# Seven of eight experts: tokens turned to columns, and results turned back, by VectorE's 32x32 block transposes instead of TensorE's, with the rows taken by way of DRAM

## The chip, the cores and the metric

The kernel runs on one core of one Trainium2 chip. The metric is the device time of one execution in microseconds (us); the figure for the kernel before is the median of 3 runs.

## What is computed

An attention readout gives 4352 tokens of 512 features. They go through a gated feed-forward layer, and its result, `x` below, through a layer of 8 experts, each of which takes 544 tokens (`cap`):

```python
logits = x @ w_gate                      # 4352 x 8
order = np.argsort(-logits.flatten())
for idx in order:                        # best scores first
    tok, e = int(idx) // E, int(idx) % E
    if assigned[tok] >= 0 or counts[e] >= cap: continue
    assigned[tok] = e; counts[e] += 1
for e in range(E):
    mask = assigned == e
    h = np.maximum(x[mask] @ w1[e], 0.0)   # 512 -> 1024
    out[mask] = h @ w2[e]                  # 1024 -> 512
```

## The kernel before

Phases 1 and 2 (attention, gated layer, its output projection, and the routing) leave two things: the rows of `x` in DRAM (`yd`, 4352 x 512) and a table `idx` with, for each expert, the numbers of its 544 tokens in five blocks (four of 128 and one of 32). The change touches phase 3, the experts, one after the other.

Products are taken with split operands: each operand is a high and a low part, and three matmuls (high x high, high x low, low x high) stand for one. So every operand of a matmul is cast once by ScalarE (ACT, the high part) and subtracted once by VectorE (DVE, the low part); `split` does both.

For one expert:
- **gather** (L959 on): GpSimd (POOL) reads each block of rows by an indirect DMA into `row` (5 buffers). TensorE (PE) turns each block into columns with 4 transposes into PSUM, `pt` (L976; 20 for an expert). ACT and DVE split `pt` into `thi` and `tlo`.
- **up** (L981 on): for each of 8 feature blocks and two token ranges (256 and 288 columns) PE does 12 matmuls into `pu` (L994, 3 PSUM banks); ACT writes `uhi` (L996) and DVE `ulo` (L997). Here the next expert's gather is run in steps (`beside`).
- **down** (L1015 on): the tokens from 256 on are computed features by tokens, 4 feature blocks of 24 matmuls of 288 columns each, into `pd` (L1026), and copied by ACT to `sw`. The first 256 tokens are computed tokens by features, 2 blocks of 24 matmuls of 512 columns (L1038).
- **swapped** (L1045 on): PE turns `sw` back to rows with 12 transposes (L1052). **scatter** copies a block of rows to `o` (L1007, ACT or DVE by turns) and POOL stores the rows at their places in the output by an indirect DMA (L1008).
- **weights**: `load` (L853) issues 512 KB of weights on SyncE's (SP) queue into `raw` (3 buffers), and `weight` splits it into a ring of 12 `w` tiles (L66 on ACT, L67 on DVE). An expert takes four such tiles for `w1` and four for `w2`.

A scheduler orders the instructions of each engine in this phase by simulated times. Each engine and each queue then works through its own list in order, and waits on semaphores.

Of the kernel before, what the change touches and what calls it, by code (L numbers as in the profile page):

```python
# [9 lines left out]
F32 = mybir.dt.float32  # L10
F32R = mybir.dt.float32r
BF16 = mybir.dt.bfloat16
I32 = mybir.dt.int32
# [4 lines left out]
OP = mybir.AluOpType  # L18
# [6 lines left out]
DM, FF = 512, 1536  # L25
E, F2 = 8, 1024
CAP = N // E
# [18 lines left out]
def some(steps, n):  # L46
    for _ in range(n):
        next(steps, None)


def whole(steps):
    for _ in steps:
        pass


class Program:
# [923 lines left out]

    def up(self, x, w, beside):  # L981
# [4 lines left out]
        for f in range(8):  # L986
# [12 lines left out]
            if 0 < f < 7:  # L999
                some(beside, 1)  # L1000
        whole(beside)
        return hi, lo

    def scatter(self, e, i, n, pd):
        nc = self.nc
        o = self.op.tile([128, DM], F32, name="o", bufs=4)
        (nc.vector.tensor_copy if i % 2 else nc.scalar.copy)(o[:n], pd[:n])  # L1007
        st = nc.gpsimd.indirect_dma_start(  # L1008
            out=self.out, in_=o[:n], in_offset=None,
            out_offset=bass.IndirectOffsetOnAxis(ap=self.idx[:n, 5 * e + i:5 * e + i + 1], axis=0))  # L1010
        for other in self.stores:
            self.tc.declare_no_dep(st.ins, other.ins, reason="rows of other tokens")
        self.stores.append(st)

    def down(self, e, x, w):  # L1015
# [3 lines left out]
        sw = self.op.tile([128, 4, CAP - T], F32, name="sw", bufs=1)  # L1019
        for fb in range(4):  # L1020
# [8 lines left out]
            nc.scalar.copy(sw[:, fb], pd)  # L1029
# [12 lines left out]
        if e < E - 1:  # L1042
            self.swapped(e, sw)
# [12 lines left out]
    def phase3(self):  # L1056
        tc, nc, a = self.tc, self.nc, self.a
        with ExitStack() as ctx:
# [10 lines left out]
            self.turned = self.turn  # L1069
            for e in range(E):  # L1070
                x2 = self.up(x, w1, self.gather(e + 1, more) if e + 1 < E else iter(()))
# [5 lines left out]
                self.down(e, x2, w2)  # L1077
# [3 lines left out]
    def run(self, out):  # L1081
        tc, nc = self.tc, self.nc
        self.out = out
        with ExitStack() as ctx:
# [6 lines left out]
            self.yd = dp.tile([N, DM], F32, name="yd")  # L1091
            with ExitStack() as pools, ExitStack() as first:
                self.phase1(pools, first)
                self.phase2(pools, first, ctx)
# [3 lines left out]
def layout(i):  # L1098
# [20 lines left out]
    w1 = i["moe2_w1"].reshape(E, 4, 128, 4, 256)  # L1119
    o["w1"] = c(w1.transpose(0, 3, 2, 1, 4).reshape(E, 4, 128, 1024))  # L1120
    w2 = i["moe2_w2"].reshape(E, 4, 2, 128, DM)
# [16 lines left out]
    o["ident"] = np.eye(128, dtype=f)  # L1138
    o["cst"] = np.concatenate([np.asarray(parts[n], f) for n, _, _ in CONSTS], 1)
# [16 lines left out]
```

## Time and profile before

| | |
|---|---|
| median of 3 runs | 1313.41 us (1312.94 to 1313.56) |
| the profiled execution | 1317.34 us |
| its span, first to last instruction | 1315.5 us |
| mean granted clock of TensorE | 0.978 |
| busy in the span | PE 1253.0 us, weight loads (PEld) 1006.5, DVE 803.9, ACT 557.6, POOL 230.1 |

The profiled execution is 3.93 us above the median. Shares are averages over phases with different limits; the experts take about the last 430 us. Where a row gives a time, it counts from the start of the span.

### The profile page before, as it was taken

The page shows a single profiled execution, that of the slowest core. Times are in us where ns is not written, and L with a number is a line of the kernel's source. Part 1 is how long each engine was busy: PE and PEld are TensorE (multiplying, and loading weights), DVE is VectorE, ACT ScalarE, POOL GpSimd, SP SyncE. Part 2 cuts the span into 40 slices and gives each one's busy share as a digit, 9 for nine tenths or more (in the row PEclk, how much of TensorE's full clock was granted, in tenths as well). Part 3 has the DMA queues.
Part 4 walks back from the last instruction along what each step waited for, and adds up shares of the span by engine and source line. Part 5 has one row for each costly group of instructions (what it writes and reads, how often), then busy time and mean ns, then how long its engine had stood idle before and what let it go on. Part 6 is the DMA issues. An engine that isn't in the chain of part 4 may idle for free.

```text
span 1315.5 us, 21466 instructions
## 1 busy us (share of the span) xinstructions
PE 1253.0 (95%) x8351; PEld 1006.5 (77%) x8351; DVE 803.9 (61%) x1673; ACT 557.6 (42%) x975; POOL 230.1 (17%) x205
## 2 busy tenths in 40 slices
PE   5888999999999999999999999979999999999997
PEld 2556768777775555877777777759999999999996
DVE  7999998778553332469889989745335344253220
ACT  4878876787642232431212121224334334343221
POOL 5754451222100000000000000033112112021011
PEclk9788999999999999999999999989999999999999
DMA  7554566345454574643333333347335244253000
GB/s 265 176 166 148 169 190 175 105 157 161 135 145 132 163 198 131 227 137 113 120 106 119 107 115 110 105 133 226 119 102 164 90 139 139 69 170 131 1 35 34
DMA packets 132885, 178.50 MB, mean 136 GB/s; under 512 B 9648, under 2 KB 99888, under 8 KB 132784
## 3 DMA queue, kind: packets, MB, share of 16 engines
q1 hardware_dynamic: 127152, 159.30, 38.6%
q0 software_dynamic: 5632, 17.83, 4.1%
q8 instruction: 66, 1.08, 0.4%
q14 instruction: 35, 0.29, 0.1%
HBM read 129.38 MB, written 47.71 MB: 135 GB/s over the span
## 4 chain that ended last, share of the span: by engine, by line
PE 56%; issue 22%; DVE 11%; DMA 4%; POOL 4%; ACT 2%; SPq 0%; POOLq 0%; ACTq 0%; DVEq 0%
PE pp L274 20%; PE pp L893 17%; PE ps_x L251 4%; PE pu L994 3%; PE ps_s L313 2%; POOL out L1008 2%; DMA raw<-w 2%; PE pd L1026 2%; PE ps_l L313 2%; POOL row L968 2%; PE pd L1038 1%; DVE slo L262 1%; PE ps_s L658 1%; DVE hlo L871 1%; DVE cvc L93 1%
## 5 line engine op out<-in xcount | busy, mean ns | idle before, releaser
L893 PE MATMUL pp<-w,hhi 128*128 128x512 f32 x816 | 261.7, 398 | 0.0
L994 PE MATMUL pu<-thi,w 128*128 128x256 f32 (+1 forms) x1024 | 209.0, 291 | 0.9 <-DVE ulo L997 0.6
L893 PEld LDWEIGHTS pp<-w,hhi 128*128 128x128 f32 x816 | 151.5, 188 | 33.8 <-issue 2.5
L274 PE MATMUL pp<-ahi,shi 128*128 128x512 f32 x384 | 159.2, 415 | 9.1 <-ACT shi L258 4.5
L994 PEld LDWEIGHTS pu<-thi,w 128*128 128x128 f32 x1024 | 166.3, 189 | 1.6 <-DVE ulo L997 0.8
L893 PE MATMUL pp<-w,hlo 128*128 128x512 f32 x408 | 162.4, 398 | 1.3 <-DVE hlo L871 1.3
L262 DVE TENSOR_TENSOR slo<-ps_x,shi 64x512 fp32r<-64x512 f32 x192 | 132.0, 687 | 40.3 <-ACT shi L258 37.2
L274 PE MATMUL pp<-ahi,slo 128*128 128x512 f32 x384 | 151.3, 403 | 3.4 <-DVE slo L262 3.4
L274 PE MATMUL pp<-alo,shi 128*128 128x512 f32 x384 | 153.8, 401 | 0.7 <-POOL alo L67 0.7
L994 PE MATMUL pu<-tlo,w 128*128 128x288 f32 (+1 forms) x512 | 148.8, 291 | 0.0
L881 ACT CAST hhi<-hlo 128x768 fp32r<-128x768 f32 x68 | 53.4, 833 | 221.1 <-PE pp L893 212.2
L67 DVE TENSOR_TENSOR w<-raw,w 128x1024 fp32r<-128x1024 f32 x56 | 68.8, 1228 | 117.8 <-ACT w L66 111.1
L280 DVE TENSOR_TENSOR ht<-pp,sg 128x512 f32<-128x512 f32 (+1 forms) x108 | 71.3, 660 | 113.1 <-PE pp L274 80.3
L258 ACT CAST shi<-ps_x 64x512 fp32r<-64x512 f32 x192 | 111.5, 581 | 57.9 <-PE ps_x L251 52.3
L997 DVE SCALAR_TENSOR_TENSOR ulo<-pu,uhi 128x256 fp32r<-128x256 f32 (+1 forms) x128 | 56.0, 439 | 100.4 <-ACT uhi L996 93.7
L274 PEld LDWEIGHTS pp<-ahi,shi 128*128 128x128 f32 x384 | 73.5, 192 | 46.4 <-ACT sg L278 9.7
L1026 PE MATMUL pd<-uhi,w 128*128 128x288 f32 x512 | 107.5, 298 | 0.0
L278 ACT ACTIVATE sg<-pp 128x512 f32<-128x512 f32 (+1 forms) x108 | 62.0, 575 | 94.0 <-PE pp L274 92.9
L996 ACT ACTIVATE uhi<-pu 128x256 fp32r<-128x256 f32 (+1 forms) x128 | 50.8, 398 | 117.6 <-PE pu L994 104.0
L994 PEld LDWEIGHTS pu<-tlo,w 128*128 128x128 f32 x512 | 96.9, 189 | 0.1
L274 PEld LDWEIGHTS pp<-ahi,slo 128*128 128x128 f32 x384 | 73.8, 192 | 27.0 <-DVE slo L262 9.4
L893 PEld LDWEIGHTS pp<-w,hlo 128*128 128x128 f32 x408 | 76.8, 188 | 18.0 <-DVE hlo L871 1.7
(235 smaller groups left out, 2231.2 us busy)
## 6 DMA issues: line engine op xcount, KB each, us to landing
raw<-w SPq DMA_DIRECT2D x64, 512.0 KB, 3.3
hlo<-hd SPq DMA_DIRECT2D x34, 768.0 KB, 4.3
hd<-ht SPq DMA_DIRECT2D x96, 256.0 KB, 2.6
hraw<-hd SPq DMA_DIRECT2D x144, 128.0 KB, 3.2
raw<-wgv SPq DMA_DIRECT2D x24, 512.0 KB, 5.0
yd<-ys SPq DMA_DIRECT2D x32, 256.0 KB, 3.3
xt<-xt SPq DMA_DIRECT2D x12, 512.0 KB, 5.4
xn<-xn SPq DMA_DIRECT2D x12, 512.0 KB, 4.5
```

What stands on the lines that cost most here:

```text
L67: lo_engine.tensor_tensor(lo, src, hi.bitcast(F32), OP.subtract)
L251: nc.tensor.matmul(ps[:, 256 * g:256 * g + 256], ss[:, 2 * g + z, :], wf[:, ws, :, 2 * g + z, :], start=i == 0, stop=i == 2)
L258: nc.scalar.copy(hi[r[z], b], banks[z][q])
L262: nc.vector.tensor_tensor(lo[r[z], b], banks[z][q], hi[r[z], b].bitcast(F32), OP.subtract)
L274: nc.tensor.matmul(pp, w(ws, k, m), xx[:, k, :], start=i == 0, stop=i == 3 * kt - 1)
L278: nc.scalar.activation(sg, pg, AF.Silu)
L280: nc.vector.tensor_tensor(ht, pv, sg, OP.mult)
L881: nc.scalar.copy(hi[:, q], raw[:, q])
L893: nc.tensor.matmul(py, x[:, f, :], wo[f // 2][:, f % 2, ws, :], start=i == 0, stop=i == 3 * NF - 1)
L994: nc.tensor.matmul(pu, wf[:, ws, k, cs], x[xs][:, k, q], start=i == 0, stop=i == 11)
L997: nc.vector.scalar_tensor_tensor(lo[:, f, q], pu, 0.0, hi[:, f, q].bitcast(F32), op0=OP.max, op1=OP.subtract)
L1026: nc.tensor.matmul(pd, wf[:, ws, f % 2, 128 * fb:128 * fb + 128], xs[:, f, T:], start=i == 0, stop=i == 23)
```

## The change

For experts 1 to 7, `fetch` takes the place of `gather`. The rows are gathered as before, but then SP stores them to a DRAM buffer `xg` and reads them back by 20 smaller DMAs into another arrangement: partition t of quarter z holds, for the tokens t, t+32, ..., the 128 features of quarter z. On this DVE's block transpose, which turns each 32x32 block in its place, gives columns. They have their features in another order within a 128-row tile; the host permutes the rows of `w1` for experts 1 to 7 to match.

For experts 0 to 6, DVE's block transpose also takes `pd` of the 288-column part straight from PSUM to `sw`, where 32 tokens then stand with a quarter row (128 features) on each partition. POOL stores them as 9 indirect DMAs of quarter rows, by a table `idx4` (4 times the row number, plus the quarter) that is made once. The host permutes the columns of `w2`, and the copy to `o` undoes this for the tokens below 256. Expert 0's gather and expert 7's way back stay as they were.

```diff
+    def fetch(self, e, x):
+        nc = self.nc
+        hi, lo = [self.tp.tile([128, 4, CAP], F32R, name=n) for n in ("thi", "tlo")]
+        x[:] = hi, lo
+        xg = self.xg[e - 1]
+        blocks = [(slice(128 * i, min(128 * i + 128, CAP)), min(128, CAP - 128 * i)) for i in range(5)]
+        for i, (q, n) in enumerate(blocks):
+            row = self.tp.tile([128, DM], F32, name="row", bufs=5)
+            nc.gpsimd.indirect_dma_start(
+                out=row[:n], out_offset=None, in_=self.yd,
+                in_offset=bass.IndirectOffsetOnAxis(ap=self.idx[:n, 5 * e + i:5 * e + i + 1], axis=0))
+            nc.sync.dma_start(xg[q], row[:n])
+        yield
+        four = []
+        for q, n in blocks:
+            four.append(self.tp.tile([128, DM], F32, name="row", bufs=5).rearrange("p (b c) -> p b c", c=128))
+            for z in range(4):
+                nc.sync.dma_start(four[-1][32 * z:32 * z + 32, :n // 32],
+                                  xg[q, 128 * z:128 * z + 128].rearrange("(b t) c -> t b c", t=32))
+        yield
+        for (q, n), t in zip(blocks, four):
+            turned = self.tp.tile([128, 4, 128], F32, name="turned")
+            nc.vector.transpose(turned[:, :, :n].rearrange("p f (b c) -> p f b c", c=32),
+                                t[:, :n // 32].rearrange("p b (f c) -> p f b c", c=32))
+            self.split(hi[:, :, q], lo[:, :, q], turned[:, :, :n], nc.vector)
+            yield
@@ up
-            if 0 < f < 7:
+            if f in (1, 4):
                 some(beside, 1)
-        whole(beside)
@@ scatter
-        (nc.vector.tensor_copy if i % 2 else nc.scalar.copy)(o[:n], pd[:n])
+        (nc.vector.tensor_copy if i % 2 else nc.scalar.copy)(
+            o[:n].rearrange("p (q f c) -> p f q c", q=4, c=32), pd[:n].rearrange("p (f q c) -> p f q c", q=4, c=32))
@@ down
+        turned = sw.rearrange("p f c -> p (f c)").rearrange("p (b c) -> p b c", c=128)
...
-            nc.scalar.copy(sw[:, fb], pd)
+            if e == E - 1:
+                nc.scalar.copy(sw[:, fb], pd)
+            else:
+                nc.vector.transpose(turned[:, :, 32 * fb:32 * fb + 32], pd.rearrange("p (b c) -> p b c", c=32))
+            some(beside, 1)
+        if e < E - 1:
+            quarters = self.out.rearrange("n (q c) -> (n q) c", q=4)
+            for b in range((CAP - T) // 32):
+                i = 5 * e + 2 + b // 4
+                self.store(quarters, turned[:, b], self.idx4[:, b % 4, i:i + 1])
         for t in range(2):
...
             self.scatter(e, t, 128, pd)
-        if e < E - 1:
-            self.swapped(e, sw)
+            some(beside, 1)
+        whole(beside)
@@ phase3
+            four, self.idx4 = [self.op.tile([128, 4, 5 * E], I32, name=n, bufs=1) for n in ("four", "idx4")]
+            quarter = self.op.tile([128, 1], F32, name="quarter", bufs=1)
+            nc.sync.dma_start(quarter, a["quarter"])
+            for z in range(4):
+                for b in range(4):
+                    nc.sync.dma_start(four[32 * z:32 * z + 32, b], self.idx[32 * b:32 * b + 32])
+            nc.vector.tensor_scalar(self.idx4, four, 4.0, quarter, op0=OP.mult, op1=OP.add)
```

`store` is the second half of the old `scatter` under its own name.

The lists of the engines move with it. On PE, at the end of an expert in steady state (`pd` of the 512-column part, then `pu` of the next expert), the list before reads:

```order
L1038 MATMUL pd<-w,uhi 128x512 x2
L1038 MATMUL pd<-w,ulo 128x512
L1052 MATMUL pt<-ident,sw 128x128 x8
L994 MATMUL pu<-thi,w 128x256
L994 MATMUL pu<-tlo,w 128x256
L994 MATMUL pu<-thi,w 128x256 x2
```

and the list of the changed kernel, at the same place:

```order
L1079 MATMUL pd<-w,uhi 128x512 x2
L1079 MATMUL pd<-w,ulo 128x512
L1023 MATMUL pu<-thi,w 128x288
L1023 MATMUL pu<-tlo,w 128x288
L1023 MATMUL pu<-thi,w 128x288
L1023 MATMUL pu<-thi,w 128x256
L1023 MATMUL pu<-tlo,w 128x256
```

The 8 transposes of `sw` are gone. The first two `pu` groups of the next expert (all 12 matmuls of one, 9 of the other) have moved ahead, into this expert's `down`, so only the 3 last matmuls of the second stand behind `pd` before the third `pu` begins.

On DVE, in expert 0, the list before, from the second `ulo`'s neighbours on (`w` is the low part of a weight tile):

```order
L997 SCALAR_TENSOR_TENSOR ulo<-pu,uhi 128x256
L67 TENSOR_TENSOR tlo<-pt,thi 128x4x32
L67 TENSOR_TENSOR tlo<-pt,thi 128x4x128
L997 SCALAR_TENSOR_TENSOR ulo<-pu,uhi 128x256
L67 TENSOR_TENSOR w<-raw,w 128x1024
L997 SCALAR_TENSOR_TENSOR ulo<-pu,uhi 128x288
L67 TENSOR_TENSOR w<-raw,w 128x1024
```

and of the changed kernel:

```order
L1026 SCALAR_TENSOR_TENSOR ulo<-pu,uhi 128x256
L67 TENSOR_TENSOR tlo<-pt,thi 128x4x32
L1117 TENSOR_SCALAR idx_9633<-four,quarter 128x160
L1026 SCALAR_TENSOR_TENSOR ulo<-pu,uhi 128x256
L1026 SCALAR_TENSOR_TENSOR ulo<-pu,uhi 128x288 x2
L1005 STREAM_TRANSPOSE turned<-row 128x512
L1026 SCALAR_TENSOR_TENSOR ulo<-pu,uhi 128x256
L67 TENSOR_TENSOR tlo<-turned,thi 128x4x128
L1005 STREAM_TRANSPOSE turned<-row 128x512
```

The block transposes of expert 1 (`turned`) now stand between the `ulo` of expert 0, and the weights' low parts have moved behind them.

On SP the list before is, through all experts, only loads of weights. In the changed kernel, in steady state (`xg_89` is one expert's DRAM buffer):

```order
L994 DMA xg_89<-row 128x512 x2
L853 DMA raw<-w 128x1024 x3
L994 DMA xg_89<-row 128x512
L853 DMA raw<-w 128x1024
L994 DMA xg_89<-row 128x512
L853 DMA raw<-w 128x1024
L1000 DMA row<-xg_89 32x4x128 x4
L994 DMA xg_89<-row 32x512
```

The loads of weights now stand in one queue with stores that wait for a gather, and with the reads back.

## Rows read from the trace of the kernel before

**Rows 1.** Windows: busy us (instructions) of each engine, PE clock, DMA share, GB/s
```profile
894.00:915.00 21.00, 20.21 (x158) 19.77 (x159) 13.87 (x23) 11.58 (x22) 6.96 (x6) 1.00 0.82 271
1102.00:1154.00 52.00, 52.00 (x370) 49.37 (x370) 20.58 (x31) 19.73 (x37) 9.54 (x10) 1.00 0.39 125
```

**Rows 2.** Timeline of POOL: start, duration, instruction [idle before <- releaser]
```profile
1043.05 1.01 POOL L1008 DMA_INDIRECT out<-o,idx  x1 [25.69 <-ACT o L1007]
...
1102.21 0.98 POOL L1008 DMA_INDIRECT out<-o,idx  x1 [0.31 <-issue]
1103.49 0.98 POOL L1008 DMA_INDIRECT out<-o,idx  x1 [0.30 <-issue]
...
1146.88 1.01 POOL L1008 DMA_INDIRECT out<-o,idx  x1 [25.70 <-ACT o L1007]
```

**Rows 3.** Timeline of PE in one steady expert, same columns; xN is N in a run
```profile
1091.77 0.62 PE L1038 MATMUL pd<-w,uhi 128*128 128x512 f32 x2
...
1098.72 0.62 PE L1038 MATMUL pd<-w,uhi 128*128 128x512 f32 x2
...
1100.53 0.40 PE L994 MATMUL pu<-thi,w 128*128 128x256 f32 x2
...
1101.23 0.40 PE L994 MATMUL pu<-thi,w 128*128 128x256 f32 x2
...
1105.04 0.28 PE L994 MATMUL pu<-thi,w 128*128 128x256 f32 x1
1105.16 0.60 PE L976 MATMUL pt<-ident,row 128*128 128x128 f32 x4
...
1105.72 0.30 PE L994 MATMUL pu<-tlo,w 128*128 128x288 f32 x1
...
1131.28 0.43 PE L1026 MATMUL pd<-uhi,w 128*128 128x288 f32 x2
...
1132.48 0.56 PE L1026 MATMUL pd<-uhi,w 128*128 128x288 f32 x3
```

**Rows 4.** Tile pt: xcount, ns min/median/max, first and last start us, forms
```profile
L976 PE MATMUL pt<-ident,row x160: 220/272/477, 884.7 to 1223.6; 128*128 128x128 f32 x128, 32*128 32x32 f32 x32
...
L1052 PE MATMUL pt<-ident,sw x96: 270/272/273, 944.7 to 1304.8; 128*128 128x128 f32 x64, 128*32 128x128 f32 x32
```

**Rows 5.** DVE's groups by shape: count | busy us, mean ns | idle before, releasers
```profile
L67 DVE TENSOR_TENSOR w<-raw,w 128x1024 fp32r<-128x1024 f32 x56 | 68.8, 1228 | 117.8 <-ACT w L66 111.1 <-PE pu L994 5.7
...
L997 DVE SCALAR_TENSOR_TENSOR ulo<-pu,uhi 128x288 fp32r<-128x288 f32 x64 | 29.2, 456 | 56.5 <-ACT uhi L996 51.3 <-issue 3.3 <-ACT o L1007 1.9
...
L204 DVE STREAM_TRANSPOSE aT<-sT 128x512 f32<-128x512 f32 x12 | 8.5, 705 | 3.9 <-POOL sT L193 3.3 <-POOL alo L67 0.6
...
L1007 DVE COPY o<-pd 128x512 f32<-128x512 f32 x8 | 5.5, 686 | 24.8 <-PE pd L1038 24.8
```

**Rows 6.** DMA issues: count, size, median us from issue to landing
```profile
raw<-w SPq DMA_DIRECT2D x64, 512.0 KB, 3.3
...
hraw<-hd SPq DMA_DIRECT2D x144, 128.0 KB, 3.2
...
yd<-ys SPq DMA_DIRECT2D x8, 64.0 KB, 2.9
```

**Rows 7.** Timelines of POOL and of PE where expert 0 begins
```profile
881.12 1.15 POOL L968 DMA_INDIRECT row<-yd,idx  x1 [1.41 <-issue]
...
893.84 0.87 POOL L968 DMA_INDIRECT row<-yd,idx  x1 [1.60 <-PE pt L976]
...
884.73 1.09 PE L976 MATMUL pt<-ident,row 128*128 128x128 f32 x4 [7.98 <-DMA row<-yd,idx]
```

**Rows 8.** Timelines of SP's queue, ACT and DVE: weights in a steady expert
```profile
1103.50 0.33 SPq L853 DMA_DIRECT2D raw<-w  x1
...
1122.44 1.04 ACT L66 CAST w<-raw 128x1024 fp32r<-128x1024 f32 x1
...
1099.31 1.23 DVE L67 TENSOR_TENSOR w<-raw,w 128x1024 fp32r<-128x1024 f32 x1 [0.18 <-ACT w L66]
```

More of the change, by code (lines that the diff above doesn't have):

```diff
@@ L1006, in scatter, with store @@
         o = self.op.tile([128, DM], F32, name="o", bufs=4)
-        (nc.vector.tensor_copy if i % 2 else nc.scalar.copy)(o[:n], pd[:n])
-        st = nc.gpsimd.indirect_dma_start(
-            out=self.out, in_=o[:n], in_offset=None,
-            out_offset=bass.IndirectOffsetOnAxis(ap=self.idx[:n, 5 * e + i:5 * e + i + 1], axis=0))
+        (nc.vector.tensor_copy if i % 2 else nc.scalar.copy)(
+            o[:n].rearrange("p (q f c) -> p f q c", q=4, c=32), pd[:n].rearrange("p (f q c) -> p f q c", q=4, c=32))
+        self.store(self.out, o[:n], self.idx[:n, 5 * e + i:5 * e + i + 1])
+    def store(self, out, rows, at):
+        st = self.nc.gpsimd.indirect_dma_start(
+            out=out, in_=rows, in_offset=None, out_offset=bass.IndirectOffsetOnAxis(ap=at, axis=0))
         for other in self.stores:
@@ L1013, in scatter, with down @@
         self.stores.append(st)
-    def down(self, e, x, w):
+    def down(self, e, x, w, beside):
         nc = self.nc
@@ L1069, in phase3 @@
             self.turned = self.turn
+            four, self.idx4 = [self.op.tile([128, 4, 5 * E], I32, name=n, bufs=1) for n in ("four", "idx4")]
[5 more added lines that the diff above has]
+            nc.vector.tensor_scalar(self.idx4, four, 4.0, quarter, op0=OP.mult, op1=OP.add)
             for e in range(E):
-                x2 = self.up(x, w1, self.gather(e + 1, more) if e + 1 < E else iter(()))
+                beside = self.fetch(e + 1, more) if e + 1 < E else iter(())
+                x2 = self.up(x, w1, beside)
                 if e + 1 < E:
@@ L1076, in phase3 @@
                     x, more = more, x
-                self.down(e, x2, w2)
+                self.down(e, x2, w2, beside)
                 if e + 1 < E:
@@ L1091, in run @@
             self.yd = dp.tile([N, DM], F32, name="yd")
+            self.xg = [dp.tile([CAP, DM], F32, name=f"xg{e}") for e in range(1, E)]
             with ExitStack() as pools, ExitStack() as first:
@@ L1119, in layout @@
     w1 = i["moe2_w1"].reshape(E, 4, 128, 4, 256)
+    quarters = i["moe2_w1"].reshape(E, 4, 4, 32, 4, 256).transpose(0, 2, 1, 3, 4, 5).reshape(E, 4, 128, 4, 256)
+    w1 = np.concatenate([w1[:1], quarters[1:]])
     o["w1"] = c(w1.transpose(0, 3, 2, 1, 4).reshape(E, 4, 128, 1024))
-    w2 = i["moe2_w2"].reshape(E, 4, 2, 128, DM)
+    w2 = i["moe2_w2"].reshape(E, 4, 2, 128, 4, 4, 32).transpose(0, 1, 2, 3, 5, 4, 6).reshape(E, 4, 2, 128, DM)
     o["w2"] = c(w2.transpose(0, 1, 3, 2, 4).reshape(E, 4, 128, 1024))
@@ L1138, in layout @@
     o["ident"] = np.eye(128, dtype=f)
+    o["quarter"] = (z[:, None] // 32).astype(f)
     o["cst"] = np.concatenate([np.asarray(parts[n], f) for n, _, _ in CONSTS], 1)
```

## The prediction, made before the changed kernel ran

> **What bounds the kernel now.** I began with the windows, because shares of the whole span mix phases that have different limits. The 52 us window in the middle of the experts shows PE busy for 52.00 of 52.00 us at a granted clock of 1.00 (2.4 GHz), DVE for 20.58, ACT for 19.73, POOL for 9.54, the DMA at 0.39 [rows 1]. So one engine bounds this stage, and there is no wait to remove: time goes only by taking instructions off PE. Then the period: POOL's first store of an expert stands at 1043.05 and 1146.88, two experts apart [rows 2]; one expert takes 103.83 / 2 = 51.91 us.
>
> What of this are transposes? Starts on PE's timeline give the pitch of each kind of matmul in a run [rows 3]: 512 columns, 30 from 1091.77 to 1098.72, 0.2317 us; 256 columns, 6 in 0.70, 0.1167; 288 columns, 9 in 1.20, 0.1333. An expert has 48, 96 and 192 of them: 11.12 + 11.20 + 25.59 = 47.91 us. The rest, 51.91 - 47.91 = 4.00 us, is the 32 transposes and what it costs to switch from one kind of work to another. A direct look at one group agrees nearly: from the start of a 256-column matmul at 1105.04 to that of the second 288-column one after it at 1105.72 are 0.68 us; less the two matmuls (0.117 + 0.133) that leaves 0.43 for 4 transposes, 0.108 each [rows 3]. Thirty-two of them are 3.45 us.
>
> **What is removed.** There are 160 transposes of rows and 96 of results [rows 4], 20 and 12 in each of 8 experts. One expert's 20 (the first) and one's 12 (the last) stay, so 7 x 32 = 224 go. At 0.108 that is 24.2 us, at 4.00 an expert 28.0. I take the middle, 26, since switches between `pu` and `pd` remain and are part of the 4.00. The rows of the tile give a transpose a duration of 272 ns [rows 4], but these overlap in the pipeline; a sum with them (61 us) would count the same time more than twice. By the Trainium skill, "VectorE: DVE Perf Modes", section "The three transpose paths", TensorE takes 390 ns for a 128x128 transpose in bf16 and VectorE 311 ns, in 32x32 blocks only; its rules send the 128x128 case to TensorE. By that figure the sum would be 87 us, an estimate; the pitch here is 0.108, and the trace decides.
>
> **What is added, and what covers it.**
> - *DVE.* Five `turned` transposes for an expert, four of 128x512 and one of a quarter of that; the trace has the same operation at that shape, 705 ns [rows 5], so 4 x 0.705 + 0.2 = 3.0. Four transposes of 128x288 from PSUM: between 456 ns (a 288-column DVE operation that reads PSUM) and 705 [rows 5], 1.8 to 2.8. One `o` copy goes (0.69) [rows 5]. DVE goes from 20.6 to about 25 of 48 us: covered by PE's stream. The split now reads SBUF and not PSUM; I take its cost as unchanged. ACT loses 4 copies and two of the `o` copies, POOL's 3 indirect stores become 9, for 6 more.
> - *POOL.* An indirect DMA of 128 rows occupies it for 0.98 at a pace of 1.28 (1102.21, 1103.49) [rows 2]; one of 32 rows for 0.87 [rows 7]. So it is counted by instruction and hardly by rows, and a quarter-row store of 128 pieces should take about the same: 6 more are 7.7 us, 17 of 48. Covered.
> - *SP and DMA.* 25 more issues for an expert at 0.33 [rows 8] are 8.3 us of queue time. A store has 256 KB and a reload 64; transfers of 64, 128 and 512 KB land in 2.9, 3.2 and 3.3 [rows 6]. The bytes are 1.1 MB out and 1.1 back, 46 GB/s over 48 us on 125, so the DMA share would be 0.39 x 171 / 125 = 0.53, or more for small packets. It has been at 0.82 with PE at 20.21 of 21 [rows 1]. Covered.
> - *PE's order* at an expert's end has the first two `pu` groups moved ahead, so that 3 + 12 matmuls and 3 of `pd`, 15 x 0.125 + 3 x 0.133 = 2.3 us, stand behind the last 512-column block. DVE's part there: the low half of a weight tile that ends 1.13 after PE (1099.31 + 1.23 [rows 8] against 1098.72 + 3 x 0.2317 [rows 3]), `o` 0.69 and `ulo` 0.46 [rows 5], 2.3. So it is near even, and I give the steady boundaries 0 to 0.3 us each, in sum 0 to 2, and take 0.
>
> **What is given back.** In expert 0 nothing has been made ready ahead. The last gather of the second expert stands at 893.84, and a gather takes 3.6 from its start until PE uses it (881.12 to 884.73) [rows 7]; so the last store is issued at 897.4, 20 reloads go behind it on the queue by 904, and landing at 2.9 [rows 6] makes the blocks complete at about 901.5, 902.8, 904, 905.5 and 906.5. The DVE list of the changed kernel puts their transposes between the `ulo` of expert 0, so an `ulo` waits behind a `turned` for which rows are still on the way, and PE has 3 `pu` banks, 4.5 us of work, ahead. I estimate 2 us of waits. The loads of the next weights have moved behind the reloads, from about 894 to 904; their casts bunch up at the first expert's end, and there DVE is behind by some 2 us (three weight halves of 1.23 [rows 5] and a `turned` ahead of `o`). I take 1.8. Together 3.8, from 0 (PE's buffers cover all) to 10 (two weights and two blocks in a chain at both places).
>
> **The sum** against the profiled execution: 1317.34 - 26 + 3.8 = 1295.1 us. It stands 3.93 above the median of the runs, so 1291.2; I say 1291. The ends of the two terms give 1317.34 - 28 + 0 - 3.93 = 1285.4 and 1317.34 - 24.2 + 10 - 3.93 = 1299.2.
>
> **The rivals.**
> 1. *More is given back at the beginning and at the boundaries.* Waits of 1 to 2 us at each of the 6 steady boundaries (DVE and PE are within 0.1 of each other there) and 5 in expert 0: 10 to 20 back, so 1297 to 1307. For it: DVE's list is in order and gains 4 to 5 us of work. Against: DVE would be busy for half of the time only.
> 2. *Slower: weights late behind GpSimd's stores.* In the SP list the `w2` loads stand behind the third store to `xg`, which waits for a gather, which stands on POOL behind nine quarter-row stores. Nine at 1.28 are 11.5 us from the end of the 288-column part, at about 1089 of the steady expert shown (48 matmuls of 0.2317 before 1099.4 [rows 3]), and the gather and its landing then put the loads at about 1105.4. Before, the load was issued at 1103.50 and converted at 1122.44 [rows 8]; with 3.3 for landing [rows 6] 15.6 us of slack, 13.7 of which would remain. It decides from (11.5 + 13.7) / 9 = 2.8 us for a store; to lose 3.7 us an expert and with that the whole gain, 3.2; at 4 us for a store the wait is 10.8 us an expert, the result 1291 + 7 x 10.8 = 1367. Against: 0.98 [rows 2], and 0.87 at a quarter of the rows [rows 7].
> 3. *Slower: reloads that land late.* A reload has about 22 us from issue to use in a steady expert, an estimate from its place in the two lists; if the pieces of 512 bytes landed in 26 us and not 3, PE would wait 4 us an expert and the gain would be gone; at 32 us it would wait 10 in each of 6 and some 29 in expert 0, where nothing covers it, 1291 + 89 = 1380, and each further us costs 7 more. Against: loads of 128 KB land in 3.2 [rows 6], and each piece read here is 128 adjacent features. The Trainium skill ("DMA: Bandwidth & Descriptors", section "Rules for kernel authors") speaks against a transpose by a plain DMA with a rearranged pattern: 19 times slower than the hardware transpose. By that, on 3.2, the landing would be 61 us and the kernel about 1580, an estimate. I give it little, since the DMA here moves whole pieces and DVE turns the elements; no row of the trace before has such a reload.
> 4. *No change:* waits of 26 us in sum, 3.7 an expert, in whatever place. Nothing in the profile speaks for just that size.
>
> **How the numbers follow.** My forecast 0.72 (1285.5 to 1297); rival 1 0.18 (1297 to 1307), rival 2 0.05, rival 3 0.02, rival 4 0.03. The range 1285.5 to 1299 holds the forecast and the nearest part of rival 1, some 0.8. Within 0.2% of 1313.41, which is about what a measurement of this kernel can tell from no change, is 1310.8 to 1316.0: rival 4 and little else, 0.03. Faster 0.90 (the forecast and rival 1), slower 0.07 (rivals 2 and 3).
>
> **What would show it.** In the profile of the changed kernel: 20 transposes of rows and 12 of results left on PE; a period of 47.9 to 48.4 us between POOL's first stores of two experts in place of 51.91; PE still busy for all of a steady window at clock 1.00, DVE near half. DVE's transposes at 0.7 and 0.45 to 0.7, a quarter-row store near 1 us, reloads landing in about 3, the DMA share at 0.5 to 0.65. PE idle by some 4 us in all between 894 and 950, ended by `ulo` or other DVE work. I would be wrong if PE idles at every expert's end, or waits for a weight tile, or if the period does not fall by 3.4 to 4.

## The result, and the profile after

The changed kernel takes 1303.57 us (median of 5 runs, 1297.39 to 1307.10), the kernel before 1313.56 in the runs beside it: a ratio of 0.9913, 95% interval 0.9886 to 0.9939. It is faster, by less than half of what I forecast: 10 us and not 22, and outside the range of 1285.5 to 1299.

The profiled executions differ by more, 1317.34 to 1303.84. This does not lie in the work. GpSimd's last store starts at 1307.15 before and at 1297.98 after, 9.2 us apart, and the rest is the time that the program takes to end behind it:

```profile
1307.15 0.98 POOL L1008 DMA_INDIRECT out<-o,idx  x1 [0.31 <-issue]
```

```profile
1297.98 0.99 POOL L1040 DMA_INDIRECT out<-o,idx  x1 [0.31 <-DVE o L1035]
```

(The first row is the timeline of POOL before, the second that after.) So 9.2 is the number to explain, and it agrees with the medians. Of it 1.3 were won ahead of the experts: the first gather stands at 879.84, before at 881.12 [rows 7]. The experts themselves gained 7.9.

What was removed and added is as costed. The view of tile pt after, the first group that answers to [rows 4], shows 20 and 12 transposes left on PE:

```profile
L976 PE MATMUL pt<-ident,row x20: 221/421/476, 883.6 to 891.1; 128*128 128x128 f32 x16, 32*128 32x32 f32 x4
...
L1093 PE MATMUL pt<-ident,sw x12: 271/272/273, 1289.8 to 1295.7; 128*128 128x128 f32 x8, 128*32 128x128 f32 x4
```

The groups of DVE from 876 us on (as [rows 5]) and the tile view of the quarter-row stores (min/median/max ns):

```profile
L1005 DVE STREAM_TRANSPOSE turned<-row 128x512 f32<-128x512 f32 x28 | 19.5, 696 | 13.7 <-DMA row<-xg 13.5
...
L1064 DVE STREAM_TRANSPOSE sw<-pd 128x288 f32<-128x288 f32 x28 | 12.1, 455 | 16.8 <-PE pd L1058 13.0 <-issue 3.8
```

```profile
L1040 POOL DMA_INDIRECT out<-sw,idx x63: 967/972/1706, 943.0 to 1247.3; - x63
```

The transposes take 0.70 and 0.455 us, a store of 128 quarter rows 0.97, all near what I took. And where nothing disturbs it, an expert takes what it should. The windows of the changed kernel (columns as in [rows 1]):

```profile
946.00:998.00 52.00, 46.14 (x306) 43.86 (x305) 24.69 (x41) 15.43 (x29) 22.69 (x22) 0.90 0.69 222
998.00:1046.00 48.00, 47.42 (x332) 44.70 (x331) 23.69 (x39) 16.09 (x29) 16.23 (x15) 1.00 0.57 179
1046.00:1094.00 48.00, 46.98 (x328) 44.32 (x328) 23.70 (x39) 17.27 (x30) 15.22 (x15) 1.00 0.55 173
1142.00:1190.00 48.00, 48.00 (x338) 45.88 (x337) 22.60 (x37) 17.38 (x30) 12.14 (x12) 1.00 0.33 112
```

In the last of these PE is busy for all of 48.00 us. In the first it lost 5.9 us, and its clock fell to 0.90. Before, it was busy for all of every such window. PE's timeline gives the period. The last 512-column matmul ends an expert:

```profile
946.02 0.39 PE L1079 MATMUL pd<-w,ulo 128*128 128x512 f32 x1
...
1001.09 0.39 PE L1079 MATMUL pd<-w,ulo 128*128 128x512 f32 x1
...
1051.36 0.39 PE L1079 MATMUL pd<-w,ulo 128*128 128x512 f32 x1
...
1101.54 0.39 PE L1079 MATMUL pd<-w,ulo 128*128 128x512 f32 x1
...
1151.82 0.39 PE L1079 MATMUL pd<-w,ulo 128*128 128x512 f32 x1
...
1199.82 0.39 PE L1079 MATMUL pd<-w,ulo 128*128 128x512 f32 x1
```

The differences are 55.07, 50.27, 50.18, 50.28, 48.00. An expert has 192 matmuls of `pu`, but PE's list moves some of them over an end: the first period holds 174 and the second 196, the three behind them 192. At 0.125 us each an undisturbed first period would be 45.8 and the second 48.5. So 9.3 us are lost at the first boundary between two experts, 1.8, 2.2 and 2.3 at the next three, nothing at the one behind them, and (from the pitches in the same timeline) 1.95 at the last. Together 17.5. In expert 0, from its first transpose to its end, PE's time above its pitches is 8.3 us, and was 6.7 before: 1.7 more. That makes 19.2 us given back, where I had 3.8. The gain without them would be 7.9 + 19.2 = 27.1; I had 26.

**The first boundary.** DVE's timeline there:

```profile
947.90 0.71 DVE L1005 STREAM_TRANSPOSE turned<-row 128x512 f32<-128x512 f32 x1 [7.05 <-DMA row<-xg]
948.54 2.32 DVE L67 TENSOR_TENSOR w<-raw,w 128x1024 fp32r<-128x1024 f32 x2
950.77 0.70 DVE L1005 STREAM_TRANSPOSE turned<-row 128x512 f32<-128x512 f32 x1
951.40 1.18 DVE L67 TENSOR_TENSOR w<-raw,w 128x1024 fp32r<-128x1024 f32 x1
952.51 0.68 DVE L1035 COPY o<-pd 128x512 f32<-128x512 f32 x1
```

DVE stood for 7.05 us ahead of a block transpose whose reload was on its way, and behind it waited three weight halves and the copy `o` that frees PE's third `pd` buffer. That block is the eleventh, so it belongs to expert 3, two experts later than the one about to begin: the scheduler had let the fetches run ahead, and put this transpose where its simulated reload had landed. PE and its clock (timeline of PE, then windows):

```profile
953.24 0.61 PE L1058 MATMUL pd<-uhi,w 128*128 128x288 f32 x1 [3.92 <-DVE o L1035]
```

```profile
948.00:952.00 4.00, 0.85 (x2) 0.50 (x2) 4.00 (x5) 0.70 (x3) 3.05 (x3) 0.56 0.79 214
952.00:956.00 4.00, 2.76 (x11) 2.72 (x12) 2.21 (x5) 0.96 (x1) 3.22 (x3) 0.50 0.98 306
956.00:960.00 4.00, 4.00 (x24) 4.00 (x23) 1.99 (x3) 1.43 (x3) 3.09 (x3) 0.66 0.92 286
```

PE had stood for 1.94 us just before these windows' first matmul, at 948.48, and the clock fell there to 0.50 (1.2 GHz). After the wait of 3.92 PE got that clock for some 5 us more, so the two waits cost more than their length.

**The later boundaries.** Here DVE was not late. The timelines of ACT, PE and DVE at the fourth boundary:

```profile
1105.44 0.39 ACT L1025 ACTIVATE uhi<-pu 128x256 fp32r<-128x256 f32 x1 [0.84 <-remote]
1110.52 0.41 ACT L1025 ACTIVATE uhi<-pu 128x288 fp32r<-128x288 f32 x1 [4.69 <-PE pu L1023]
```

```profile
1105.84 0.41 PE L1023 MATMUL pu<-thi,w 128*128 128x288 f32 x2
...
1109.65 0.29 PE L1023 MATMUL pu<-thi,w 128*128 128x288 f32 x1
1111.47 0.39 PE L1023 MATMUL pu<-thi,w 128*128 128x256 f32 x1 [1.53 <-DVE ulo L1026]
```

```profile
1110.96 0.46 DVE L1026 SCALAR_TENSOR_TENSOR ulo<-pu,uhi 128x288 fp32r<-128x288 f32 x1 [4.67 <-ACT uhi L1025]
```

ACT had done its `uhi` of 1105.44 by 1105.83 and stood idle for 4.69 us for the next. Its list holds nothing between the two. The `pu` that it wanted was done: the row at 1105.84 holds the twelfth matmul of that group and the first of the next. PE went on for two more groups, filled its three buffers and stopped at 1109.9. Only at 1110.5 did ACT get going, then DVE, then PE. So ACT took the group up 4.7 us after its last matmul began. Elsewhere ACT follows in 0.3 to 0.5. The profile names "PE pu" as what ended the wait, but PE's row does not say that PE was late; one has to set the group's own last matmul beside it.

The trace also keeps the time of every update of a semaphore, and these settle whether PE's update was late or ACT slow to see it. The last matmuls of the three groups end at 1106.14, 1107.55 and 1109.94 (ends of matmuls are modelled); PE's updates for them stand at 1110.49, 1110.62 and 1110.80, that is 4.35, 3.07 and 0.86 later. From the end of expert 0 on no update of DVE or of ACT comes later than 0.02 us, in this run or in any other. So it was PE's update that was late. (Where the views name "remote" as what ended ACT's wait, it was such an update of PE too: 1105.42 for the row at 1105.44, 1.67 late.) The late ones come in one go, here 1.2 us after GpSimd's string of indirect DMAs at this expert's end, 11 stores and two gathers, was over (1109.30). Before there is a trace of the same thing, once an expert, and it cost nothing. ACT's row there, for the group whose last matmul is the row of 1105.04 in [rows 3]:

```profile
1106.73 0.38 ACT L996 ACTIVATE uhi<-pu 128x256 fp32r<-128x256 f32 x1 [2.14 <-PE pt L976]
```

That is 1.7 late; the update stands at 1106.71, 1.1 us after GpSimd's four stores in a row.

### The profile page after: what moved, and what is told of

It is laid out like the page before. It is cut to its first block, busy times and chain, and to the rows that moved or that the text cites. A ratio compares the mean times of both kernels' runs of the same rounds, so it can differ in the third digit from the quotient of the medians.

```text
span 1302.0 us, 21367 instructions
## 1 busy us (share of the span) xinstructions
PE 1230.8 (95%) x8127; PEld 984.4 (76%) x8127; DVE 827.2 (64%) x1730; ACT 541.4 (42%) x933; POOL 281.1 (22%) x247
## 4 chain that ended last, share of the span: by engine, by line
PE 70%; DVE 12%; issue 7%; DMA 5%; ACT 2%; POOL 2%; SPq 1%; another core or an unknown queue 1%; POOLq 0%; DVEq 0%; ACTq 0%
PE pp L274 20%; PE pp L893 17%; PE pu L1023 11%; PE pd L1058 6%; PE pd L1079 4%; PE ps_x L251 4%; PE ps_s L313 2%; PE ps_l L313 2%; DVE slo L262 1%; DMA raw<-w 1%; POOL out L1040 1%; DVE cvc L93 1%; PE ps_s L658 1%; DVE hlo L871 1%; DVE cvt L85 1%
## 5 line engine op out<-in xcount | busy, mean ns | idle before, releaser
L1023 PE MATMUL pu<-thi,w 128*128 128x256 f32 (+1 forms) x1024 | 211.8, 293 | 4.7 <-ACT thi L66 2.4
L1023 PEld LDWEIGHTS pu<-thi,w 128*128 128x128 f32 x1024 | 169.4, 192 | 6.9 <-ACT thi L66 2.5
L274 PE MATMUL pp<-ahi,shi 128*128 128x512 f32 x384 | 159.7, 417 | 10.4 <-ACT shi L258 6.7
L1040 POOL DMA_INDIRECT out<-sw,idx x63 | 66.9, 1062 | 113.1 <-DVE sw L1064 95.7
```

The costliest lines, as they stand in the source:

```text
L274: nc.tensor.matmul(pp, w(ws, k, m), xx[:, k, :], start=i == 0, stop=i == 3 * kt - 1)
L1023: nc.tensor.matmul(pu, wf[:, ws, k, cs], x[xs][:, k, q], start=i == 0, stop=i == 11)
L1040: st = self.nc.gpsimd.indirect_dma_start(out=out, in_=rows, in_offset=None, out_offset=bass.IndirectOffsetOnAxis(ap=at, axis=0))
```

## Experiments

All ratios are to the kernel before, with 95% intervals. The table counts periods as above (end of an expert to the end of the next), worked out from each run's PE timeline, beside the first what PE lost in it by its pitches (the first periods do not all hold the same matmuls), and last the greatest time, in the 10 us after ends 1 to 3, from the start of a group's last matmul to ACT's `uhi`. This last column counts whatever ACT waited for, late weights too.

| run | ratio | first | lost in it | next three | last | ACT late, us |
|---|---|---|---|---|---|---|
| changed kernel | 0.9913 | 55.07 | 9.3 | 50.27, 50.18, 50.28 | 49.45 | 4.5, 4.9, 4.7 |
| e1 hold | 0.9915 | 53.99 | 6.8 | 49.71, 49.78, 49.82 | 47.93 | 3.5, 3.6, 3.6 |
| e2 rows only | 0.9932 | 55.84 | 7.1 | 49.23, 49.30, 49.29 | 49.36 | 3.1, 1.0, 0.9 |
| e3 back only | 0.9921 | 50.87 | 1.7 | 51.01, 49.57, 51.01 | 49.48 | 1.5, 1.6, 1.5 |
| e4 three stores | 0.9879 | 55.37 | 8.8 | 48.03, 48.00, 48.00 | 47.53 | 2.6, 2.3, 2.1 |
| e5 late gathers | 0.9892 | 53.21 | 4.3 | 50.79, 48.78, 49.81 | 47.88 | 4.0, 2.6, 4.1 |
| e6 first gather | 0.9821 | 55.14 | 7.8 | 48.62, 48.31, 48.01 | 49.35 | 3.5, 3.5, 3.5 |
| e7 pieces on SP | 0.9942 | 55.80 | 8.4 | 52.16, 49.98, 51.81 | 47.53 | 5.3, 4.6, 4.9 |
| e8 tiny stores | 1.0219 | 54.93 | 9.1 | 56.43, 55.62, 57.67 | 51.50 | 6.3, 6.8, 7.7 |
| e9 five buffers | 0.9854 | 52.93 | 4.9 | 48.75, 48.31, 48.03 | 49.92 | 4.1, 4.3, 2.8 |
| e10 five, first gather | 0.9832 | 51.29 | 3.3 | 48.03, 48.39, 48.03 | 50.03 | 2.8, 4.2, 2.8 |
| e11 five, hold | 0.9796 | 48.19 | 0.2 | 48.03, 48.23, 48.03 | 49.88 | 2.8, 4.2, 3.5 |
| e12 four buffers | 0.9901 | 54.60 | 7.1 | 48.03, 48.03, 48.03 | 49.23 | 2.8, 2.7, 2.6 |

Without loss a period is 48.0 where all transposes of an expert are gone, and about 1.3 more in e2 (12 transposes at 0.108) and 2.2 more in e3 (20). In e3 a group of 12 matmuls stands by turns on either side of an end (198 and 186 matmuls of `pu` in its periods), so 51.01 and 49.57, with a mean of 50.29, are both without loss. The last column of periods holds expert 7, whose own way back is unchanged.

**e1, order on VectorE.** The copy to `o` that ends an expert is kept in `self.fin`, and the block transposes are queued behind it:

```diff
-            nc.vector.transpose(turned[:, :, :n].rearrange("p f (b c) -> p f b c", c=32),
-                                t[:, :n // 32].rearrange("p b (f c) -> p f b c", c=32))
+            with self.tc.issue_after(self.fin) if e > 1 else ExitStack():
+                nc.vector.transpose(turned[:, :, :n].rearrange("p f (b c) -> p f b c", c=32),
+                                    t[:, :n // 32].rearrange("p b (f c) -> p f b c", c=32))
```

> The changed kernel, with one thing moved: on VectorE's list, the block transposes of the next expert but one stand behind the copy to o that ends an expert, and not ahead of it. Theory A (order on VectorE): at the first boundary the changed kernel lost 7.1 us (55.07 between the ends of experts 0 and 1 where an undisturbed expert took 48.0), because o, two weight halves and then PE waited behind a turned whose reload was on its way; without that the 7.1 falls to 0 to 2, the granted clock stays at 1.00 between 946 and 970, and the ratio to before is 0.986 to 0.988. Theory B (semaphore updates of PE arrive late behind GpSimd's string of indirect DMAs) says nothing of the first boundary; the next three keep their loss of about 2.2 us each. Rival C (the DMA engines are full, whatever the order): the first boundary loses 5 or more still, ratio 0.991.

0.9915 (0.9902 to 0.9929), no gain. The wait of 7 us for the reload is gone, but the first boundary still loses 6.8, and the steady ones 1.7: two `turned` now stand ahead of the first `ulo`, and PE waits for that one. The rows of PE at the second boundary of e1:

```profile
1000.31 0.68 PE L1061 MATMUL pd<-uhi,w 128*128 128x288 f32 x3
1002.11 0.40 PE L1024 MATMUL pu<-thi,w 128*128 128x288 f32 x1 [1.12 <-DVE turned L1006]
```

At the first boundary PE's updates are late in their turn: the last matmul of a group ends at 952.99, its update stands at 958.76, and ACT's row is

```profile
958.78 0.41 ACT L1026 ACTIVATE uhi<-pu 128x288 fp32r<-128x288 f32 x1 [2.52 <-remote]
```

Theory A as I put it, that this order alone is the 7 us, is refuted.

**e2 and e3, each half alone.** e2 takes back the stores of quarter rows and the transposes from PSUM (`down`, `scatter` and `w2` as before). e3 keeps these, and gathers and turns rows as before.

> Only the first half of the change: rows by way of DRAM and VectorE's transposes, results back by PE's transposes and stores of whole rows as before. 84 PE transposes are back, 1.5 us an expert. Theory B: GpSimd's string at an expert's end is 5 stores again and not 11, so the steady boundaries lose under 0.5 us each where the changed kernel lost 2.2, period 49.5 to 49.8 in place of 50.2. Theory A: the first boundary still loses 5 to 8 us. Together about 1307, ratio 0.994. Rival C (DMA traffic, above all stores and reloads): the steady boundaries lose 2 us as before, period 51.5 or more, ratio 0.999 to 1.002.

> Only the second half: rows gathered and turned by PE as before, results back by VectorE from PSUM and stored by quarter rows. 84 PE transposes are gone, 1.5 us an expert. Theory B: the string of 11 indirect stores and the gathers behind it is there, so the boundaries lose about 2 us, period 51.9 to 52.5, and nothing is gained: ratio 0.998 to 1.002. Theory A: no loss of 7 us at the first boundary, as no turned stands on VectorE's list. Rival C (stores to DRAM and reloads fill the DMA): without them the boundaries lose nothing, period 50.4, ratio 0.992.

e2: 0.9932 (0.9919 to 0.9945), as expected: the steady boundaries lose nothing, the first 7.1. e3: 0.9921 (0.9908 to 0.9935), better than I expected. Its steady boundaries lose nothing either, though GpSimd has the same 9 stores in a string; PE's updates are late there by 1.2 to 1.6, which its other buffers cover. So the string of stores alone does not bring the loss at those boundaries, nor do fetches alone: either half gives 8.7 to 10.4 us, both together 10. In e2 the first boundary shows one more wait. ACT's row there:

```profile
954.61 1.05 ACT L66 CAST w<-raw 128x1024 fp32r<-128x1024 f32 x1 [8.93 <-DMA raw<-w]
```

The load of that weight was issued at 948.79, behind eight reloads on SP's queue: the wait that I had named for the steady state, at another place.

**e4, e7, e8, what makes the updates late.** In all three the results from token 256 on go to other rows or nowhere; that part of the output is left out. e4 stores the same bytes in 3 indirect DMAs of 2 KB rows; e7 adds to it, on SP, 9 plain DMAs of 128 pieces of 512 bytes; e8 adds instead, on GpSimd, 6 indirect DMAs of 8 pieces each. First e4's diff, then the lines that stand ahead of its own loop in e7 and in e8:

```diff
-            for b in range((CAP - T) // 32):
-                i = 5 * e + 2 + b // 4
-                self.store(quarters, turned[:, b], self.idx4[:, b % 4, i:i + 1])
+            for t in range(2, 5):
+                n = min(128, CAP - 128 * t)
+                self.store(self.out, wide[:n, 512 * (t - 2):512 * (t - 2) + 512] if t < 4 else wide[:n, 640:1152],
+                           self.idx[:n, 5 * e + t:5 * e + t + 1])
```

```diff
+            for b in range(9):
+                nc.sync.dma_start(self.scr[128 * b:128 * b + 128, :128], turned[:, b])
```

```diff
+            for b in range(6):
+                i = 5 * e + 2 + b // 4
+                self.store(self.scr, turned[:8, b], self.idx4[:8, b % 4, i:i + 1])
```

> The changed kernel, with the same number of bytes of the part from token 256 on stored by 3 indirect DMAs of rows of 2 KB in place of 9 of 512 bytes. What is stored are not the rows of the result, that part of the output is left out; all waits on sw stay. Theory B (it is the number of indirect DMAs in GpSimd's string): the steady boundaries lose under 0.5 us, period 48.0 to 48.5, late updates of PE's semaphore under 2 us, ratio 0.985 to 0.988 with the first boundary's loss kept. Rival C (bytes of the DMA): boundaries as in the changed kernel, period 50.2, ratio 0.991.

> The kernel with 3 stores of whole rows in place of 9 of quarter rows (the results from token 256 on are not the right rows, this part of the output is left out), and beside them 9 plain DMAs on SP's queue that write the same 1152 pieces of 512 bytes to a scratch buffer. It has the DMA engines' small pieces without GpSimd's instructions. Theory B (GpSimd's string): steady periods stay at 48.0 to 48.6. Rival E (small pieces load the DMA engines, and this delays PE's updates): periods 49.5 to 50.5, late updates of 2 to 5 us after the boundary.

> The same kernel with 3 stores of whole rows (the same part of the output is left out), and ahead of them 6 indirect stores on GpSimd of only 8 pieces of 512 bytes each, to a scratch buffer. It has the 9 instructions of the string without their bytes. Theory B (GpSimd's string counts): steady periods 49.5 to 50.5 if these stores take about 0.9 us each as one of 32 rows does, with PE's updates late by 2 to 5 us. Rival E (small pieces): 48.0 to 48.5.

e4: 0.9879 (0.9861 to 0.9897); every steady loss is gone, also the last. From the end of expert 0 on no update of PE that its trace holds (a few per cent of such records are missing) is later than 0.01 us; the 2.1 to 2.6 in the table are ACT's waits for weights (one of 2.00 us up to 1056.75). Its first boundary lost 8.8 all the same, with the wait for `o` as in the changed kernel:

```profile
953.42 0.61 PE L1058 MATMUL pd<-uhi,w 128*128 128x288 f32 x1 [3.49 <-DVE o L1035]
```

The window of one expert of e4:

```profile
1050.10:1098.10 48.00, 48.00 (x337) 45.88 (x336) 23.59 (x39) 17.39 (x31) 9.92 (x10) 1.00 0.56 179
```

The DMA share of an expert is 0.56, in the changed kernel 0.52 to 0.57: rival C, that the load of the DMA engines does it, is refuted.

e7 (0.9942, 0.9927 to 0.9957) loses time again, but by another wait. PE's updates are on time in it (none later than 0.16 us from the end of expert 0 on). What ACT stood for, and with it PE's groups behind, is a weight; its rows at the second and the third boundary:

```profile
1011.33 1.04 ACT L66 CAST w<-raw 128x1024 fp32r<-128x1024 f32 x1 [5.08 <-DMA raw<-w]
...
1062.65 1.05 ACT L66 CAST w<-raw 128x1024 fp32r<-128x1024 f32 x1 [4.33 <-DMA raw<-w]
```

So plain DMAs of small pieces do not make PE's updates late, and rival E is refuted too. e8 (1.0219, 1.0202 to 1.0237) does: five updates of PE that were due from 1113.06 to 1116.27 stand at 1121.00 to 1121.27, 2.4 us after GpSimd's string of 12 was over (1118.55). They hold even ACT's weights, as a cast waits until PE is done with the tile that it overwrites:

```profile
1006.91 1.04 ACT L66 CAST w<-raw 128x1024 fp32r<-128x1024 f32 x1 [4.58 <-DMA raw<-w]
1009.06 0.69 ACT L1025 ACTIVATE uhi<-pu 128x256 fp32r<-128x256 f32 x2 [1.11 <-remote]
...
1121.02 1.04 ACT L66 CAST w<-raw 128x1024 fp32r<-128x1024 f32 x1 [5.98 <-remote]
```

At 1006.9 the weight and PE's update (1006.84, 5.8 late) came at the same instant; at 1121.0 the weight had landed by 1114.0. So theory B stands: it is GpSimd's indirect DMAs, counted by instruction and hardly by bytes. Why e8, with as many of them as the changed kernel, loses 6 to 9 us an expert and not 2 is not shown.

**e5 and e6, when the fetches run.** e5 lets the gathers of experts 2 to 7 wait for the second `uhi` block of the expert before; e6 turns expert 1's rows on PE, as expert 0's, and begins to fetch with expert 2. The diff of e5 (`g` is the gather, `self.mark` that `uhi` block), then that of e6:

```diff
+            if e >= 2:
+                self.tc.add_manual_dep(g.ins, self.mark.ins.name, mybir.DependencyInfo(
+                    mybir.DependencyClass.Sync, mybir.DependencyReason.DATA), reason="not before this expert")
```

```diff
-                beside = self.fetch(e + 1, more) if e + 1 < E else iter(())
+                beside = (self.fetch if e else self.gather)(e + 1, more) if e + 1 < E else iter(())
```

> The changed kernel, but from expert 2 on the five gathers of an expert's rows wait for the second feature block of the expert before it. So in expert 0 only one fetch runs and not a second and part of a third, the block transposes stand in the lists of the expert that has time for them, and GpSimd's string at an expert's end is 11 stores without two gathers in it. Theory D (crowding: a fetch too early costs at the first boundary, and gathers in the string cost at the others): first boundary 48 to 50 and not 55.07, the others 48.0 to 48.5 and not 50.2, time 1288 to 1293, ratio 0.980 to 0.984. If the string's 9 quarter-row stores alone are enough (theory B as first put): others 49.5 to 50.2. Rival: rows come too late now, and PE waits for a thi or a turned at each expert's start: periods over 51, ratio over 0.993.

> The changed kernel, with expert 1's rows turned by PE as expert 0's are; fetch begins with expert 2. 20 PE transposes are back in expert 0, 2.5 us. Theory D (two fetches and part of a third crowd expert 0): the start and the first boundary lose under 3 us together where they lost about 10, the other boundaries as in the changed kernel, 50.2; time 1296 to 1299, ratio 0.986 to 0.989. If the first boundary is only VectorE's list: it loses 5 or more still, ratio 0.993.

e5: 0.9892 (0.9877 to 0.9908), 1301.01. A miss: of the next three periods two are better, by 0.5 and 1.4, and one is worse by 0.5; PE now waits some 10 us later for an `ulo`, the fifth period is 51.23 where it was 48.00, and the first boundary still loses 4.3. e6: 0.9821 (0.9806 to 0.9836), 1292.04, better than the 1296 to 1299 that I gave it; but the trace is of its slowest execution (1299.15 where the others took 1289 to 1292), and in that one the first boundary lost 7.8 through late updates and a slow clock. So e6 shows that a better place for the fetches is worth some 12 us, and its trace does not show where. Its steady boundaries cost 0 to 0.6 with ACT late by 3.5: what is lost begins there.

**e9 to e12, more buffers for PE.** If ACT is late by a time that cannot be helped, PE needs something to do. `pst` has two PSUM banks that after the change serve only expert 0 and expert 7. e9 gives both to `pu` (the few transposes left use `pd`); e10 adds e6, e11 adds e1; e12 gives one.

```diff
-            self.pst = ctx.enter_context(tc.tile_pool(name="pst", bufs=2, space=PSUM))
-            self.psu = ctx.enter_context(tc.tile_pool(name="psu", bufs=3, space=PSUM))
+            self.psu = ctx.enter_context(tc.tile_pool(name="psu", bufs=5, space=PSUM))
```

> The changed kernel with five PSUM buffers for pu in place of three; the two that pt had are not needed between expert 1 and 6, and the transposes of expert 0 and 7 that are left take a buffer of pd. Theory F (at an expert's end ACT sees PE's update 3.3 to 4.9 us late; two other pu buffers cover two groups of 12 matmuls, 1.4 to 1.6 us each, about 3.1; what is over stands PE still): four others cover 6 us, so the loss of 2.2 us at three boundaries and of 1.9 at the last falls under 0.3 each, periods 48.0, while the late updates themselves stay at 3 to 5 us. The first boundary keeps most of its 7. Time 1294 to 1298, ratio 0.984 to 0.988. If the loss is order on VectorE or a late weight, buffers do not help: periods 50.2, ratio 0.991.

> The same five buffers, and expert 1's rows turned by PE in expert 0. In the run with that alone the three boundaries lost 0 to 0.6 and the first 7.1, with updates of PE up to 9 us late. Theory F: the first boundary falls from 7.1 to about 4 (3 us more are covered), the last loses under 0.3 instead of 1.9; time 1285 to 1289, ratio 0.978 to 0.981. If not: 1292, ratio 0.982.

> The same five buffers, and on VectorE's list the transposes of the next expert but one behind the copy that ends an expert. With that order alone every boundary lost 1.4 to 1.8 us, as PE waited for the first ulo behind two turned. Theory F: with two more buffers PE has 3 us more to do there, the losses of 1.4 to 1.8 go, and the first falls from 6.0 to 3; time 1290 to 1294, ratio 0.981 to 0.985. If not: 1302, ratio 0.991.

> The changed kernel with four PSUM buffers for pu (three before) and one for pt (two before), the dose between the changed kernel and the run with five; pd is untouched. Theory F: three other buffers cover 4.6 us, so updates that come 4.5 to 4.9 us late cost 0 to 0.4 us at the three boundaries and the last, where they cost 1.7 to 2.3 with three buffers and 0 to 0.7 with five; the first boundary keeps 4 to 7. Time 1295 to 1299, ratio 0.985 to 0.989. If the gain of the run with five buffers came from its other order and not from buffers: boundaries of about 2, 1303, ratio 0.991.

e9: 1293.72 us, 0.9854 (0.9825 to 0.9883); e10: 1292.99, 0.9832 (0.9819 to 0.9845); e11: 1287.90, 0.9796 (0.9782 to 0.9810), the best version, 27 us below the kernel before; e12: 1301.17, 0.9901 (0.9884 to 0.9918). The clean comparison is the last boundary, where ACT is late by much the same time in all of them. ACT in the changed kernel, then ACT, POOL and PE in e11:

```profile
1252.72 0.99 ACT L1025 ACTIVATE uhi<-pu 128x288 fp32r<-128x288 f32 x3 [5.12 <-PE pu L1023]
```

```profile
1232.98 0.96 ACT L1026 ACTIVATE uhi<-pu 128x256 fp32r<-128x256 f32 x3 [10.16 <-PE pu L1024]
```

```profile
1228.89 0.97 POOL L1043 DMA_INDIRECT out<-o,idx  x1 [0.31 <-issue]
1230.17 0.97 POOL L1043 DMA_INDIRECT out<-o,idx  x1 [0.30 <-issue]
```

```profile
1228.90 0.41 PE L1024 MATMUL pu<-thi,w 128*128 128x256 f32 x2
...
1232.30 0.43 PE L1024 MATMUL pu<-thi,w 128*128 128x288 f32 x2
1232.94 0.30 PE L1024 MATMUL pu<-tlo,w 128*128 128x288 f32 x1 [0.22 <-issue]
```

The first of the three groups that ACT takes at 1232.98 was done at 1228.9. PE went on to 1232.7 and lost about 0.4 us. The changed kernel, late by 4.4 there, lost 1.95; e12, late by 4.0, lost 0.3; e4, where PE's updates are on time, lost 0.1. At the three boundaries before, e12 loses nothing, but ACT is also less late in it (2.7), so there the other order has its part. e11 keeps all six periods from the first within 0.25 of 48.0, with a window of the first expert behind the first boundary that is full:

```profile
938.80:987.00 48.20, 48.20 (x338) 45.98 (x336) 25.97 (x41) 18.42 (x33) 18.84 (x17) 1.00 0.59 193
```

The misses: e10 and e12 took 4 and 2 us more than I had given them, e11 2 less. e10 came out where I had put it if buffers do nothing, and no faster than e6 (0.9832 against 0.9821), though its first boundary lost 3.3, near what was expected: the two gains do not add up. e12 is not clearly faster than the changed kernel (0.9901 and 0.9913, the intervals overlap); its single `pt` costs 2.9 us in expert 0, and its first boundary lost 7.1.

## Why the prediction was wrong

1. *What is removed*: right. 26 predicted, 27.1 found, between the two ends of 24.2 and 28.0. PE's pitch, and not the duration of a row, was the right price. The Trainium skill's 390 ns for a transpose ("VectorE: DVE Perf Modes", section "The three transpose paths") would have given 87, and the trace does not agree with it as a price here.
2. *What is added*: the prices were right (0.70, 0.455, 0.97 us; DVE 23.7 and POOL 13 to 16 of 48 busy; a DMA share of 0.52 to 0.57 where I had 0.53). A reload was quick: the four DMAs of the first block begin at 897.22, some 0.46 apart on SP's timeline, and its transpose began at 901.17, so it landed within 2.6 us of the last of them. The one that DVE stood for at 947.90 took longer, 5.3 from the last issue before it at 942.59. Rival 3 did not come about. The Trainium skill's rule on rearranged patterns ("DMA: Bandwidth & Descriptors", section "Rules for kernel authors") would have given 61, an estimate, and the trace does not agree with it for these pieces of 512 adjacent bytes.
3. *Expert 0*: 2 us predicted, 1.7 found, near by luck, for the cause was another: PE waited 2.4 us from 891 on for a `thi` that stood on ACT behind a late update (893.15 for a matmul that ended at 890.99 by its row), and not for a `turned` ahead of an `ulo`. The rows of ACT and PE:

```profile
893.17 0.38 ACT L1025 ACTIVATE uhi<-pu 128x256 fp32r<-128x256 f32 x1 [2.45 <-remote]
...
893.76 0.76 PE L1023 MATMUL pu<-thi,w 128*128 128x288 f32 x2 [2.40 <-ACT thi L66]
```

4. *The first boundary*: mis-sized, 1.8 predicted, 9.3 found. I had the right place and the right engine, a `turned` and weights ahead of `o` on DVE. What I did not do was to ask of each `turned` in that list for which expert it is and when its reload is issued; it was one of expert 3, with a reload issued 5 us ahead. And several waits lay one under the other there: e4 has no late update and still lost 8.8, e1 mends the order and lost 6.8 with an update 5.8 late, and only e11, with the order and the buffers, lost 0.2.
5. *The steady boundaries* are the step whose mechanism failed: "it is near even, and I give the steady boundaries 0 to 0.3 us each, in sum 0 to 2, and take 0". I weighed DVE's work against PE's and found 2.3 on both sides. DVE was in time. What was late was PE's own update, so that ACT took up a group 4.5 to 4.9 us after its last matmul began, against some 3.0 us of other `pu` buffers (two groups of 12 matmuls at 0.117 and 0.133). The sum of that, with the last boundary, is 8.2 us. It comes with GpSimd's indirect stores, nine where three were; I had priced them as busy time of an engine with time to spare, and put at nothing what they do to others. The trace of before showed the beginning of it, ACT late by 1.7 once an expert, and I did not look for it because it cost nothing there.
6. *The rivals*: rival 1 came about, in its size (1297 to 1307) and its two places, with another mechanism. In hindsight its chance of 0.18 was too low, and a range that ended near its lower end too narrow: DVE and PE "within 0.1 of each other" was itself the warning that any further delay would show.

Left open: by what in the chip GpSimd's indirect DMAs hold PE's updates back. The runs say that with three stores in place of nine none is late (e4), that plain DMAs on SP's queue do not bring it back (e7), that nearly empty indirect ones do (e8), and that the DMA's share does not tell. How late an update comes does not go by the number of stores alone: with the same nine it is 1.2 to 1.6 at e3's steady boundaries and over 4 in the changed kernel. That buffers hide it is shown at the last boundary. At the others the lists changed with the buffers, and e9 to e12 do not part the two.

## What to carry to other kernels

Work that moves off the bounding engine takes its waits with it: cost the first round and each seam between rounds apart from the steady middle, and ask of every instruction in an in-order list which round it belongs to and when its input is issued. When a stage has no slack, look in the trace of before for delays that cost nothing yet, for these are what the change will uncover. A change that frees a resource (here two PSUM banks) pays in full only when the freed resource is given to what now waits: 10 us without it, 21 with it (e9), 27 with the order on VectorE mended as well (e11). And a wait in a trace is put down to a cause only when the semaphore's own record, or the instruction that makes the update, stands beside it: e7 and the changed kernel show ACT late by the same time, for different causes.

## What was not expected of the hardware

- TensorE's update of a semaphore can come late while GpSimd issues a string of indirect DMAs: 4.35 us after the matmul's end at 1110.49, and three groups taken up in one go at 1252.72 and at 1232.98, each 1.8 to 1.9 us after the string was over. VectorE's and ScalarE's updates are not late at the same time (at most 0.02 us).
- GpSimd's time for an indirect DMA hardly depends on what it moves: 0.97 us for 128 pieces of 512 bytes, 0.98 for 128 of 2 KB [rows 2], 0.87 for 32 of 2 KB [rows 7], 0.86 for 8 of 512 bytes (e8). Six such stores of 8 pieces, ahead of three full ones in e8, cost more than nine of 128.
- Two waits of PE, of 1.9 and 3.9 us and close together, were followed by some 5 us at half the clock.
